# Transposing q and k by crossbar DMA in place of TensorE for five of eight batches, with VectorE and SyncE held to program order

## The chip, the cores and the metric

The kernel runs on one core of one Trainium2 chip. The metric is the device time of one execution in microseconds (us). A run is called slow when it lies over 1.5% above the fastest run of the same kernel; comparisons below use fast runs. A ratio is the mean time of one kernel's fast runs over that of the other's fast runs of the same rounds, so it is not quite the ratio of the medians quoted beside it. Profiles are single executions: their spans differ by a few us from the medians (the profiled execution of the kernel before took 405.14 us, 5 us over its median).

The core has five engines with their own instruction streams. Here PE (TensorE) multiplies matrices, DVE (VectorE) and ACT (ScalarE) work element by element, POOL (GpSimd) issues the loads that convert fp32 to bf16, and SP (SyncE) issues all other DMAs.

## The reference

Attention with a causal bias, then a token and a channel mixer; 8 batches, 8 heads, 576 positions, 64 elements per head.

```python
scores = q @ k.T / sqrt(64)                     # per batch and head, 576 x 576
cum    = cumsum(maximum(s, 0))
bias   = minimum(-(cum[:, None] - cum[None, :]), 0)
attn   = softmax(where(causal, -1e9, scores + bias))
x      = (attn @ v), heads side by side          # batch x 576 x 512
u      = x + (x.T @ U @ V).T                     # mixing along the sequence, rank 32
out    = u + maximum(u @ w_ch1, 0) @ w_ch2       # mixing along the channels, 512 -> 2048 -> 512
```

## The kernel before

A *pair* is two heads of one batch; there are 32 pairs, four per batch. For each pair the kernel makes a `slot`: q and k with their 64 elements on partitions 0 to 63, and four extra rows on partitions 64 to 67 that carry the bias. These *row loads* come from DRAM by a small DMA of SyncE. q and k are loaded with positions on 72 partitions, so they have to be transposed; TensorE does that with an identity matrix into PSUM, and VectorE copies the result into the slot.

```python
def transposes(n):                       # pair n
    b, hp = divmod(n, PB)                # PB = 4 pairs per batch
    slot = slots[n % NSLOT]              # NSLOT = 5
    if b > 0:
        nc.sync.dma_start(out=slot[D:KA, :, 0 : 2 * S], in_=rows_hbm[...])     # the row load
    for hh in range(2):
        tp = pwork()...                  # a PSUM bank
        for c, src in enumerate((q_t[b], k_t[b])):
            for t2 in range(4):
                nc.tensor.transpose(tp[:, c, t2, :], src[:, h, ds(t2 * 128, 128)], identity[:TP, :TP])
        ...                              # two copies into slot[0:D, hh]
        yield
```

The channel mixer is dense TensorE work. It is cut into steps by `yield`, and the loop over pairs takes a few such steps between the steps of the attention, so that TensorE always has something to do:

```python
for n in range(PB, NP + 2):
    b, hp = divmod(n, PB)
    if hp == 0 and 1 < b < B - 1:
        load(b + 1)                      # q, k, v of the next batch, by GpSimd
    if n + 1 < NP:
        run(transposes(n + 1))
    if n < NP:
        run(scores(n))
    if hp == 1 and b > FT:
        run(seqmix(b - 1)); fill.append(chanmix(b - 1))
    if PB < n <= NP:
        run(values(n - 1))               # x of the pair; for b >= 2 also a DMA transpose xT<-x_sb
    ...
in_program_order(tc, traced, [E.Pool, E.PE])
```

What is emitted in this order is not necessarily executed in it. A scheduler in the build may reorder the instructions of an engine where the data allow it, unless `in_program_order` chains them. In the kernel before, TensorE and GpSimd are chained to the end, ScalarE, VectorE and SyncE only up to the first mixing (`in_program_order(tc, traced, [E.DVE, E.Activation, E.SP])` just before the loop).

The softmax here doesn't subtract the row's maximum and nothing guards it: scores larger than these inputs give would overflow.

## Time and profile before

| | before |
|---|---|
| median time | 400.07 us (399.89 to 408.59, 4 runs) |
| span of the profiled run | 403.4 us |
| TensorE busy | 382.8 us (95%) |
| one batch in the steady part (four pairs and a mixer) | 41.2 us |
| eight small transposes (one head) | 0.26 us |

The page of the kernel before, busy time of each engine, and the shares of the chain of work that ended last:

```profile
PE 382.8 (95%) x3525; PEld 218.2 (54%) x3525; DVE 223.3 (55%) x484; ACT 201.0 (50%) x384; POOL 56.3 (14%) x79
...
PE 82%; DMA 10%; DVE 5%; POOL 1%; issue 1%; ACT 1%; DVEq 0%; ACTq 0%
```

The busy times in four stretches of the steady part (columns: stretch, its length, then busy us and instructions of each engine, the granted TensorE clock, the DMA share, GB/s):

```profile
99.00:140.00 41.00, 40.62 (x429) 24.31 (x427) 28.76 (x57) 25.43 (x51) 5.88 (x7) 1.00 0.93 96
140.00:180.00 40.00, 39.01 (x404) 22.84 (x405) 27.41 (x59) 21.97 (x45) 5.88 (x7) 1.00 0.92 98
180.00:220.00 40.00, 39.72 (x408) 23.40 (x407) 27.31 (x58) 21.98 (x44) 5.88 (x7) 1.00 0.92 103
220.00:260.00 40.00, 39.72 (x392) 23.16 (x390) 27.06 (x57) 21.04 (x42) 5.88 (x7) 1.00 0.98 103
```

TensorE is busy for practically all of each stretch, at clock 1.00; VectorE for 27 of 40 us. So TensorE sets the time here, and work taken from it should come back as time. What one head's transposes cost it is read from the timeline, not from busy sums, which count overlapped time twice (columns: start, length, engine and line, operation):

```profile
213.12 0.29 PE L239 MATMUL pwork<-identity,q_sd 72*128 72x72 bf16 x4
213.25 0.29 PE L239 MATMUL pwork<-identity,k_sd 72*128 72x72 bf16 x4
213.38 1.03 PE L454 MATMUL pwork<-w_sb,hT 128*128 128x512 bf16 x4
214.25 0.29 PE L239 MATMUL pwork<-identity,q_sd 72*128 72x72 bf16 x4
```

From the first transpose at 213.12 to the next mixer matmul at 213.38 it is 0.26 us.

The last lines to note are those that the prediction passed over: when the row load is requested, and when it is needed. SyncE's timeline has the request:

```profile
209.81 0.24 SPq L228 DMA_DIRECT2D slot_92<-rows_hbm  x1
```

TensorE's timeline has the first matmul that reads that slot afterwards:

```profile
256.56 0.42 PE L260 MATMUL pscore<-slot_92 68*128 68x128 bf16 x5
```

The scheduler had moved the row load up to about the moment at which the slot falls free, 46.8 us ahead of its use (36 to 55 us for all 28 row loads of this trace). Nothing in the program text asks for that.

### The profile page before, as it was taken

The page shows a single profiled execution, that of the slowest core. Times are in us where ns is not written, and L with a number is a line of the kernel's source. Part 1 is how long each engine was busy: PE and PEld are TensorE (multiplying, and loading weights), DVE is VectorE, ACT ScalarE, POOL GpSimd, SP SyncE. Part 2 cuts the span into 40 slices and gives each one's busy share as a digit, 9 for nine tenths or more (in the row PEclk, how much of TensorE's full clock was granted, in tenths as well). Part 3 has the DMA queues.
Part 4 walks back from the last instruction along what each step waited for, and adds up shares of the span by engine and source line. Part 5 has one row for each costly group of instructions (what it writes and reads, how often), then busy time and mean ns, then how long its engine had stood idle before and what let it go on. Part 6 is the DMA issues. An engine that isn't in the chain of part 4 may idle for free.

```text
span 403.4 us, 8541 instructions
## 1 busy us (share of the span) xinstructions
PE 382.8 (95%) x3525; PEld 218.2 (54%) x3525; DVE 223.3 (55%) x484; ACT 201.0 (50%) x384; POOL 56.3 (14%) x79
## 2 busy tenths in 40 slices
PE   7798998798999999999999999999999999999995
PEld 3575445465555556655555565555565554444442
DVE  7875124587756775667566856785678353002011
ACT  5552479551874358534853386328642930530710
POOL 5750023320230041003200230000000000000000
PEclk9758999999999999999999999999999999999999
DMA  5999999999399359837992599251224014301002
GB/s 76 169 211 207 151 93 102 134 151 105 61 153 111 73 97 137 79 72 112 147 80 72 100 151 70 63 122 21 19 70 120 18 34 130 80 18 69 19 26 79
DMA packets 94149, 38.33 MB, mean 95 GB/s; under 512 B 77150, under 2 KB 88446, under 8 KB 94110
## 3 DMA queue, kind: packets, MB, share of 16 engines
q0 software_dynamic: 53360, 18.44, 59.8%
q1 hardware_dynamic: 40750, 19.35, 26.7%
q8 instruction: 27, 0.44, 0.5%
q14 instruction: 12, 0.10, 0.1%
HBM read 37.51 MB, written 9.95 MB: 118 GB/s over the span
## 4 chain that ended last, share of the span: by engine, by line
PE 82%; DMA 10%; DVE 5%; POOL 1%; issue 1%; ACT 1%; DVEq 0%; ACTq 0%
PE pwork L454 29%; PE pwork L442 29%; PE pscore L260 10%; DMA k_sd<-in_k_dram 7%; PE pwork L323 6%; PE pwork L239 3%; DMA v_slot_102<-in_v_dram 2%; DVE o_sb L464 1%; PE pscore L151 1%; PE pwork L395 1%; DVE x_sb L333 1%; PE pwork L352 1%; DMA hT<-in_s_dram 1%; POOL v_slot_102 L193 1%; ACT pT_87 L271 0%
## 5 line engine op out<-in xcount | busy, mean ns | idle before, releaser
L454 PE MATMUL pwork<-w_sb,hT 128*128 128x512 bf16 x576 | 142.2, 381 | 0.2 <-ACT slot_96 L245 0.2
L442 PE MATMUL pwork<-uT,w_sb 128*128 128x512 bf16 x576 | 141.0, 379 | 0.6 <-ACT slot_96 L245 0.3
L449 ACT ACTIVATE hT<-pwork 128x512 bf16<-128x512 f32 x144 | 87.8, 609 | 107.7 <-PE pwork L442 107.1
L454 PEld LDWEIGHTS <-hT 128*128 128x128 bf16 x576 | 51.8, 98 | 49.1 <-issue 0.8
L442 PEld LDWEIGHTS <-w_sb 128*128 128x128 bf16 x576 | 50.6, 98 | 47.4 <-DVE uT L377 0.7
L464 DVE TENSOR_TENSOR o_sb<-pwork,u_sd 128x512 f32<-128x512 f32 x36 | 24.9, 692 | 63.8 <-PE pwork L454 62.6
L271 ACT ACTIVATE pT_87<-pscore 128x512 bf16<-128x512 f32 x32 | 19.3, 603 | 30.7 <-PE pscore L260 30.6
L333 DVE TENSOR_TENSOR x_sb<-pwork,rec 128x320 bf16<-128x320 f32 x64 | 31.3, 490 | 2.0
L271 ACT ACTIVATE pT_86<-pscore 128x512 bf16<-128x512 f32 x32 | 19.3, 603 | 19.5 <-PE pscore L260 19.4
L99 POOL DMA_DIRECT2D q_sd<-in_q_dram x10 | 8.1, 811 | 142.1 <-PE pwork L239 126.6
L245 DVE COPY slot_96<-pwork 64x576 bf16<-64x576 bf16 x22 | 17.4, 797 | 13.9 <-PE pwork L239 13.6
L272 DVE TENSOR_TENSOR pT_87<-pT_87,keep 128x512 bf16<-128x512 bf16 x32 | 13.2, 416 | 20.5 <-ACT pT_87 L271 20.5
L272 DVE TENSOR_TENSOR pT_86<-pT_86,keep 128x512 bf16<-128x512 bf16 x32 | 13.2, 414 | 18.5 <-ACT pT_86 L271 18.4
L239 PEld LDWEIGHTS <-q_sd 72*128 72x128 bf16 x256 | 16.3, 100 | 13.2 <-DMA q_sd<-in_q_dram 1.3
L239 PE MATMUL pwork<-identity,k_sd 72*128 72x72 bf16 x256 | 19.2, 201 | 4.2 <-DMA k_sd<-in_k_dram 4.2
L377 DVE TENSOR_TENSOR uT<-pwork,xT 128x256 bf16<-128x256 f32 (+6 forms) x54 | 19.4, 418 | 6.4 <-PE pwork L395 6.4
L323 PEld LDWEIGHTS <-pT_86 128*128 128x128 bf16 x480 | 19.0, 100 | 7.2 <-issue 2.0
L332 DVE RECIPROCAL rec<-pwork 128x5 f32<-128x5 f32 x64 | 12.2, 192 | 19.2 <-PE pwork L323 18.9
L284 ACT ACTIVATE pT_87<-pscore 128x512 bf16<-128x512 f32 x32 | 19.5, 610 | 6.2 <-PE pscore L260 6.2
L284 ACT ACTIVATE pT_86<-pscore 128x512 bf16<-128x512 f32 x32 | 19.5, 611 | 4.7 <-PE pscore L260 4.6
L245 DVE COPY slot_93<-pwork 64x576 bf16<-64x576 bf16 x26 | 20.6, 796 | 2.0 <-PE pwork L239 1.6
L323 PEld LDWEIGHTS <-pT_87 128*128 128x128 bf16 x480 | 18.8, 100 | 5.3 <-DVE pT_87 L297 0.3
(100 smaller groups left out, 441.3 us busy)
## 6 DMA issues: line engine op xcount, KB each, us to landing
out_dram<-o_sb SPq DMA_DIRECT2D x36, 256.0 KB
w_sb<-in_moe_w_ch_dram POOLq DMA_DIRECT2D x2, 2048.0 KB, 20.8
q_sd<-in_q_dram POOLq DMA_DIRECT2D x7, 576.0 KB, 8.4
k_sd<-in_k_dram POOLq DMA_DIRECT2D x7, 576.0 KB, 14.0
v_slot_102<-in_v_dram POOLq DMA_DIRECT2D x12, 128.0 KB, 13.5
v_slot_103<-in_v_dram POOLq DMA_DIRECT2D x12, 128.0 KB, 15.3
v_slot_104<-in_v_dram POOLq DMA_DIRECT2D x8, 128.0 KB, 17.6
rows_hbm<-hT SPq DMA_DIRECT2D x1, 504.0 KB
```

The source lines that it names most:

```text
L239: nc.tensor.transpose(tp[:, c, t2, :], src[:, h, ds(t2 * 128, 128)], identity[:TP, :TP])
L245: copy(dst[:, :, :, :, par], tp[par * D : par * D + D].rearrange("p c t m -> p c m t"),)
L260: nc.tensor.matmul(dst, lhsT=kT[:, ds(j * 128, 128)], rhs=qT[:, lo:hi], start=True, stop=True,)
L271: nc.scalar.activation(pT[:, hh, 0:512], diag, EXP, scale=scale)
L272: nc.vector.tensor_tensor(pT[:, hh, 0:512].rearrange("p (a b) -> p a b", a=4), pT[:, hh, 0:512].rearrange("p (a b) -> p a b", a=4), keep.t ...
L284: nc.scalar.activation(pT[:, hh, 512:1024], far, EXP, scale=scale)
L323: nc.tensor.matmul(po[:, i, :], lhsT=pT[:, hh, ds(place(j, i), 128)], rhs=vt[:, j, h, :], start=(j == 0), stop=(j == i), skip_group_check= ...
L333: nc.vector.tensor_tensor(x_sb[:, hp, :, ds(hh * D, D)], po[:, :, 0:D], rec.to_broadcast([128, 5, D]), op=ALU.mult,)
L442: nc.tensor.matmul(f1, lhsT=w1_sb[:, kt, ds(nf * 128, 128)], rhs=u[:, kt, :], start=(kt == 0), stop=(kt == 3),)
L449: nc.scalar.activation(hT[:, nf, :], f1, RELU)
L454: nc.tensor.matmul(f2, lhsT=hT[:, nf, ds(i * 128, 128)], rhs=w2_sb[:, nf, :], start=(nf == 0), stop=(nf == NF - 1),)
L464: nc.vector.tensor_tensor(o_sb.rearrange("p (a b) -> p a b", a=4), f2.rearrange("p (a b) -> p a b", a=4), u_sd[:, :, i, :], op=ALU.add,)
```

## The change

The intent: take 320 of the 512 small transposes off TensorE. From batch 3 on, one DMA per pair transposes q and k through the crossbar, three pairs ahead; q and k are loaded into two fixed buffers two batches ahead. VectorE and SyncE are chained to the end, so that the copies and fetches stay where they are written. The buffers have 80 partitions, not 72: "DMA: Bandwidth & Descriptors", section "DMA Transpose (X-bar)", of the Trainium skill asks for a multiple of 16; a small DMA fills the eight spare partitions once per buffer. In the same edit two small tiles of the mixing (`uxT` and `ux`) go from two buffers to one.

```diff
+    qks = [consts.tile([TR, H, 2, TT * D], BF16, name=f"qk{i}") for i in range(2)]     # TR = 80
+    def fetch(n):
+        b, hp = divmod(n, PB)
+        qkT_of[n] = work.tile([128, 2, 2, 4, TR], BF16, tag="qkT", name="qkT", bufs=3)
+        nc.sync.dma_start_transpose(
+            out=qkT_of[n].rearrange("p a c t m -> p (a c t) m"),
+            in_=qks[b % 2][:, ds(2 * hp, 2), :, :].rearrange("p h c x -> p (h c x)"))
 ...
+            if qkT is not None:
+                tp = qkT[:, hh, :, :, :TP]            # VectorE copies from here; no TensorE
+            else:
                 ... nc.tensor.transpose ...
 ...
-    in_program_order(tc, traced, [E.DVE, E.Activation, E.SP])
+    in_program_order(tc, traced, [E.Activation])
 ...
     for n in range(PB, NP + 2):
-        if hp == 0 and 1 < b < B - 1:
-            load(b + 1)
+        if hp == 0 and 1 < b < B - 1:
+            load_v(b + 1)
+        nb = b + 2
+        if hp == (1 if b >= QT else 3) and QT <= nb < B:      # QT = 3
+            load_qk(nb, 0, H)
+        if hp == 1 and QT - 2 <= b < QT:
+            nc.sync.dma_start(out=qks[b % 2][TP:], in_=qks[b % 2][2 * TP - TR : TP])
+        if QT * PB <= n + 3 < NP:
+            fetch(n + 3)
         if n + 1 < NP:
             run(transposes(n + 1))
 ...
-    in_program_order(tc, traced, [E.Pool, E.PE])
+    in_program_order(tc, traced, [E.Pool, E.PE, E.DVE, E.SP])
```

More of the change, by code (lines that the diff above doesn't have):

```diff
@@ L70 @@
     FT = 2
+    QT = 3
     consts = ctx.enter_context(tc.tile_pool(name="consts", bufs=1))
-    loads = ctx.enter_context(tc.tile_pool(name="loads", bufs=2))
     work = ctx.enter_context(tc.tile_pool(name="work", bufs=2))
@@ L89 @@
     nc.sync.dma_start(out=s_sb, in_=s.rearrange("b h s -> (b h) s"))
-    q_t, k_t = {}, {}
-    def alloc_qk(b):
-        q_t[b] = loads.tile([TP, H, TT * D], BF16, tag="q_sd", name="q_sd")
-        k_t[b] = loads.tile([TP, H, TT * D], BF16, tag="k_sd", name="k_sd")
+    TR = 80
+    qks = [consts.tile([TR, H, 2, TT * D], BF16, name=f"qk{i}") for i in range(2)]
     def load_qk(b, h, n):
-        for dst, src in ((q_t[b], q), (k_t[b], k)):
+        for c, src in enumerate((q, k)):
             nc.gpsimd.dma_start(
-                out=dst[:, ds(h, n), :],
+                out=qks[b % 2][:TP, ds(h, n), c, :],
                 in_=src[b, ds(h, n)].rearrange("h (p t) d -> p h (t d)", p=TP),
             )
-    alloc_qk(0)
     load_qk(0, 0, 2)
@@ L169 @@
             )
-    for dst in (q_t[0], k_t[0]):
-        nc.vector.memset(dst[:, 4:8, 0:2], 0.0)
+    nc.vector.memset(qks[0][:TP, 4:8, :, 0:2], 0.0)
     load_qk(0, 4, 4)
@@ L210 @@
     nc.gpsimd.dma_start(out=w2_sb, in_=moe_w_ch2.rearrange("(kt kp) n -> kp kt n", kp=128))
-    alloc_qk(1)
     load_qk(1, 0, H)
     load_v(1)
-    uT_of, x_of, xT_of = {}, {}, {}
+    uT_of, x_of, xT_of, qkT_of = {}, {}, {}, {}
     def uT(g):
@@ L220, in uT @@
         return uT_of[g]
+    def fetch(n):
[3 more added lines that the diff above has]
+            out=qkT_of[n].rearrange("p a c t m -> p (a c t) m"),
+            in_=qks[b % 2][:, ds(2 * hp, 2), :, :].rearrange("p h c x -> p (h c x)"),
+        )
     def transposes(n):
@@ L231, in transposes @@
             )
+        qkT = qkT_of.pop(n, None)
         for hh in range(2):
             h = 2 * hp + hh
-            tp = pwork().bitcast(BF16)[:, : 2 * 4 * TP].rearrange(
-                "p (c t m) -> p c t m", c=2, t=4
-            )
-            for c, src in enumerate((q_t[b], k_t[b])):
-                for t2 in range(4):
-                    nc.tensor.transpose(
-                        tp[:, c, t2, :], src[:, h, ds(t2 * 128, 128)], identity[:TP, :TP]
-                    )
+            if qkT is not None:
+                tp = qkT[:, hh, :, :, :TP]
+            else:
+                tp = pwork().bitcast(BF16)[:, : 2 * 4 * TP].rearrange(
+                    "p (c t m) -> p c t m", c=2, t=4
+                )
+                for c in range(2):
+                    for t2 in range(4):
+                        nc.tensor.transpose(
+                            tp[:, c, t2, :],
+                            qks[b % 2][:TP, h, c, ds(t2 * 128, 128)],
+                            identity[:TP, :TP],
+                        )
             dst = slot[0:D, hh, 0 : 2 * S].rearrange("p (c m t two) -> p c m t two", c=2, t=4, two=2)
@@ L359, in seqmix @@
                 )
-        uxT = work.tile([128, 128], BF16, tag="uxT", name="uxT")
+        uxT = work.tile([128, 128], BF16, tag="uxT", name="uxT", bufs=1)
         nc.vector.tensor_copy(uxT, up)
@@ L365, in seqmix @@
         nc.tensor.matmul(up, lhsT=uxT, rhs=identity, start=True, stop=True)
-        ux = work.tile([128, 128], BF16, tag="ux", name="ux")
+        ux = work.tile([128, 128], BF16, tag="ux", name="ux", bufs=1)
         nc.vector.tensor_copy(ux, up)
@@ L515 @@
         spin(2, pscore)
-    in_program_order(tc, traced, [E.DVE, E.Activation, E.SP])
-    def load(b):
-        alloc_qk(b)
-        load_qk(b, 0, H)
-        load_v(b)
-    load(2)
+    in_program_order(tc, traced, [E.Activation])
+    load_qk(2, 0, H)
+    load_v(2)
     fill.append(chanmix(0))
```

## The prediction

> **What bounds the kernel now.** TensorE. The page has PE busy 382.8 of 403.4 us; the chain of waits is 82% PE. Busy time in windows: 140 to 184 us PE 42.8 of 44, 184 to 225 40.7 of 41, 225 to 266 40.7 of 41, 266 to 308 41.7 of 42, 308 to 343 35.0 of 35; granted clock 1.00 in all. VectorE has 28 of 41 us in such a stage, ScalarE 22. Only 0 to 98 us differs (PE 40.7 of 45 between 40 and 85, DMA engines saturated by loads). So from about 98 us on, a microsecond less of PE work is a microsecond of time, unless a new wait appears.
>
> **What goes.** 16 small transposes of each of the 20 pairs of batches 3 to 7 (320 of 512). They are pipelined, so busy time overstates them: in the timeline eight transposes occupy 213.12 to 213.38 and again 214.25 to 214.50 us, and the next four 128x512 matmuls run at their usual 0.87 us. That is 0.257 us per head; 40 heads x 0.257 = 10.3 us, all where PE is saturated. The mixer's interleaving goes by yields, whose number stays, so PE's remaining order is the same.
>
> **What comes.** 20 crossbar transposes of 80 rows x 2048 columns from SyncE; 80, because a transpose wants a multiple of 16 partitions (Trainium skill, "DMA: Bandwidth & Descriptors", section "DMA Transpose (X-bar)"; no run here shows it). The present 128x2048 transpose, when alone, busies the DMA engines for about 2.6 to 3 us and takes SyncE 1.7 to 2.3 us to issue; the 128x640 one takes about 1.0 us alone, up to 4.6 us among batch loads. By rows, my estimate for the new one is 1.7 to 2 us alone, 4 to 9 us among loads, issue 1.5 us. Three pairs ahead is 27 us (a pair takes 8.9 us in the timeline), so it should be hidden. The DMA share of a steady batch is 0.9 of 41 us, but half of that is the load burst of 18 us; four more transposes, some 8 us, fit. The skill's "Advanced Engine Details and Errata", section "X-Bar Transpose (TRN2)", expects 350 to 400 GB/s of transposes; here the DMA view shows about 210 for them, against 369 to 410 for output stores.
> VectorE's copies (797 ns from PSUM) should take 650 to 750 ns from SBUF (estimate), uncritical.
>
> **Order and loads.** GpSimd's order of loads stays; q and k buffers are freed earlier by as much as they are needed earlier. First fetch at about 98 us; batch 3's q, k have landed by 91. Program order on VectorE and SyncE follows PE's program order: small waits at most, perhaps small gains (PE loses about 4 us to VectorE after 85 us). Risks: at each batch's second pair the last transpose of x meets the load burst and the new transposes, and the mixer's evacuation waits 1 to 2 us; SyncE, blocked in order by a late load, delays row loads.
>
> **Prediction.** 400.2 - 10.3 + 0 to 2 of new waits - 0 to 2 of better order: 390.0 us, range 387 to 394. Chances: faster by over 2% 0.78, within 2% 0.19, slower 0.03.
>
> **Right if:** 320 fewer PE matmuls; pairs of batches 3 to 7 take 8.4 us; PE still 99% busy there; the 60 us of pure mixer at the end unchanged; copies wait for no DMA. **Wrong if:** VectorE copies wait for the new transposes, PE falls under 97% in a steady stage, the first 100 us change by over 2 us, or crossbar transposes take over 15 us each.

## The result

The changed kernel took 425.43 us (median of 4 runs, 419.54 to 429.14; two of them slow) against 400.07: ratio of the fast runs 1.053, 95% interval 1.044 to 1.062. It is slower by 5%, not faster by 2.6%. Its page, busy time and chain:

```profile
PE 381.7 (91%) x3205; PEld 210.0 (50%) x3205; DVE 214.5 (51%) x483; ACT 201.2 (48%) x384; POOL 57.3 (14%) x79
...
PE 69%; DMA 17%; DVE 6%; ACT 3%; issue 2%; SPq 2%; POOL 1%; ACTq 0%; DVEq 0%
```

The same four stretches of the changed kernel:

```profile
99.00:140.00 41.00, 37.09 (x322) 20.58 (x320) 24.11 (x52) 20.84 (x42) 5.88 (x7) 0.92 1.04 121
140.00:180.00 40.00, 35.27 (x330) 19.58 (x329) 24.29 (x55) 22.07 (x44) 5.88 (x7) 1.00 1.11 127
180.00:220.00 40.00, 36.19 (x301) 19.66 (x300) 22.21 (x52) 19.16 (x39) 6.26 (x7) 0.91 1.16 124
220.00:260.00 40.00, 37.38 (x330) 20.67 (x329) 25.33 (x56) 19.89 (x39) 6.27 (x7) 1.00 1.11 136
```

There are 320 fewer matmuls, as intended. But over these 161 us TensorE is busy for 145.9 us, against 159.1 before: it now waits for 15 us, where it waited for 2. In two stretches the clock is lower as well. What it waits for, from the waits of PE over the whole run (columns: us in total, times, longest), the first line of the list:

```profile
PE pscore L269 <- DMA slot<-rows_hbm: 14.0, 7, 3.8
```

The longest of these waits, in the chain of waits (start, length, what):

```profile
124.67 0.31 PE pscore L269 x3
124.98 8.19 DMA slot<-rows_hbm
133.17 0.14 issue
133.31 0.64 PE pscore L269 x5
```

The scores of a pair wait for that pair's row load, a DMA of 18 KB whose own packets take under 1 us, but which landed 8.2 us after its request. In this trace row loads are requested 3 to 14 us before their scores from pair 10 on. SyncE's timeline around it:

```profile
120.04 1.31 SPq L349 DMA_TRANSPOSE xT<-x_sb  x1
121.40 3.49 SPq L222 DMA_TRANSPOSE qkT<-qk  x1
124.98 0.49 SPq L231 DMA_DIRECT2D slot<-rows_hbm  x1
...
129.93 4.78 SPq L222 DMA_TRANSPOSE qkT<-qk  x1
134.81 0.43 SPq L231 DMA_DIRECT2D slot<-rows_hbm  x1
```

The request of 124.98 comes after a crossbar transpose of x (120.04) and one of q and k (121.40), and the packet records show those two moving their 1920 rows of 256 bytes from 123.9 to 131.2 us; the eight packets of the row load move from 131.2 to 131.9, right behind them. That fits what "DMA: Bandwidth & Descriptors", section "Two DMAs through the same engine are not ordered", says of one queue of one DMA engine: its descriptors start in order. Also, issuing the crossbar transpose held SyncE for 3.5 and 4.8 us, where the median is 1.4. So the row load was requested late, and then stood in line.

The stall has a tail. TensorE's clock right after that wait:

```profile
129.00:133.00 4.00, 0.47 (x3) 0.00 (x0) 2.14 (x4) 0.00 (x0) 0.00 (x0) 0.99 2.02 144
133.00:140.00 7.00, 6.69 (x27) 3.23 (x28) 1.68 (x4) 2.45 (x5) 0.00 (x0) 0.52 0.72 102
140.00:143.00 3.00, 3.00 (x41) 1.92 (x40) 0.69 (x2) 1.08 (x2) 1.65 (x2) 1.00 0.56 96
```

After an idle gap of 3.8 us the clock was 0.52 for the next 7 us. "TensorE: Matmul & The Clock Gate", section "What's actually happening", has the array at half clock after an idle window of about 3.4 us; this gap agrees. But a shorter one did it as well: at 209.2 us, after a stretch without a pause, TensorE waited 2.8 us for a row load, and half clock followed.

```profile
205.00:209.20 4.20, 4.20 (x42) 2.09 (x38) 3.28 (x8) 2.99 (x7) 0.00 (x0) 1.00 1.43 147
209.20:212.00 2.80, 0.03 (x1) 0.00 (x0) 0.75 (x2) 0.60 (x1) 0.00 (x0) 0.90 1.30 158
212.00:218.00 6.00, 5.93 (x26) 3.06 (x27) 0.85 (x2) 3.15 (x6) 0.00 (x0) 0.50 0.29 57
```

### The profile page after: what moved, and what is told of

The parts are those of the page before. It is cut to its first block, busy times and chain, and to the rows that moved or that the text cites. A ratio compares the mean times of both kernels' runs of the same rounds, so it can differ in the third digit from the quotient of the medians.

```text
span 417.8 us, 7944 instructions
## 1 busy us (share of the span) xinstructions
PE 381.7 (91%) x3205; PEld 210.0 (50%) x3205; DVE 214.5 (51%) x483; ACT 201.2 (48%) x384; POOL 57.3 (14%) x79
## 4 chain that ended last, share of the span: by engine, by line
PE 69%; DMA 17%; DVE 6%; ACT 3%; issue 2%; SPq 2%; POOL 1%; ACTq 0%; DVEq 0%
PE pwork L463 26%; PE pwork L451 25%; DMA slot<-rows_hbm 11%; PE pscore L269 10%; PE pwork L332 5%; DMA xT<-x_sb 3%; DMA v_slot<-in_v_dram 3%; ACT pT L297 1%; DVE o_sb L473 1%; DVE x_sb L342 1%; PE pscore L148 1%; SPq L222 1%; PE pwork L404 1%; DVE slot L254 1%; DMA hT<-in_s_dram 1%
## 5 line engine op out<-in xcount | busy, mean ns | idle before, releaser
L269 PE MATMUL pscore<-slot 68*128 68x128 bf16 (+4 forms) x576 | 70.1, 257 | 15.6 <-DMA slot<-rows_hbm 14.0
L463 PEld LDWEIGHTS <-hT 128*128 128x128 bf16 x576 | 53.9, 100 | 55.7 <-issue 3.5
L269 PEld LDWEIGHTS <-slot 68*128 68x128 bf16 x576 | 45.8, 105 | 51.1 <-DMA slot<-rows_hbm 13.6
L280 ACT ACTIVATE pT<-pscore 128x512 bf16<-128x512 f32 x64 | 38.6, 603 | 63.7 <-PE pscore L269 63.5
L281 DVE TENSOR_TENSOR pT<-pT,keep 128x512 bf16<-128x512 bf16 x64 | 26.8, 422 | 60.6 <-ACT pT L280 59.8
L254 DVE COPY slot<-qkT 64x576 bf16<-64x576 bf16 x80 | 53.8, 672 | 0.8
L332 PEld LDWEIGHTS <-pT 128*128 128x128 bf16 x960 | 37.4, 100 | 15.3 <-DVE uT L386 3.4
L293 ACT ACTIVATE pT<-pscore 128x512 bf16<-128x512 f32 x64 | 39.0, 609 | 11.4 <-PE pscore L269 11.2
L332 PE MATMUL pwork<-v_slot,pT 128*128 128x65 bf16 x960 | 39.8, 197 | 3.1 <-DMA v_slot<-in_v_dram 1.4
L297 ACT ACTIVATE pT<-pscore 128x512 bf16<-128x512 f32 x64 | 39.4, 615 | 0.0
L254 DVE COPY slot<-pwork 64x576 bf16<-64x576 bf16 x36 | 28.3, 796 | 14.4 <-PE pwork L246 13.9
L189 POOL DMA_DIRECT2D v_slot<-in_v_dram x32 | 29.1, 924 | 11.4 <-DMA v_slot<-in_v_dram 6.1
L148 PE MATMUL pscore<-busy 128*128 128x512 bf16 (+1 forms) x53 | 19.6, 467 | 1.3 <-DVE busy L124 1.3
## 6 DMA issues: line engine op xcount, KB each, us to landing
w_sb<-in_moe_w_ch_dram POOLq DMA_DIRECT2D x2, 2048.0 KB, 19.7
```

The costliest lines, as they stand in the source:

```text
L189: nc.gpsimd.dma_start(out=vt[:, t, :, 0:D], in_=v[b, :, ds(t * 128, 128), :].rearrange("h p d -> p h d"),)
L254: copy(dst[:, :, :, :, par], tp[par * D : par * D + D].rearrange("p c t m -> p c m t"),)
L269: nc.tensor.matmul(dst, lhsT=kT[:, ds(j * 128, 128)], rhs=qT[:, lo:hi], start=True, stop=True,)
L280: nc.scalar.activation(pT[:, hh, 0:512], diag, EXP, scale=scale)
L293: nc.scalar.activation(pT[:, hh, 512:1024], far, EXP, scale=scale)
L297: nc.scalar.activation(pT[:, hh, 1024:1536], mid, EXP, scale=scale)
```

## The experiments

My theory A: the loss is SyncE's program order. Row loads, which the scheduler had placed four to five pairs ahead, are now one pair ahead and behind crossbar transposes. Rivals: B, the crossbar's traffic crowds the DMA engines, whatever the order; C, VectorE's program order makes it wait for copies or masks. All twelve runs gave correct results (e10 and e12 are the same file); each was timed beside the kernel before on the same chip in 3 rounds (the last in 5).

### e1: SyncE free again, VectorE in order

```diff
-    in_program_order(tc, traced, [E.Activation])
+    in_program_order(tc, traced, [E.Activation, E.SP])
-    in_program_order(tc, traced, [E.Pool, E.PE, E.DVE, E.SP])
+    in_program_order(tc, traced, [E.Pool, E.PE, E.DVE])
```

> The changed kernel, but SyncE is held to program order only as far as in the kernel before; VectorE stays in order to the end. Theory A (SyncE's program order puts each pair's row load behind a crossbar issue that blocks for 4 to 6 us under loads): row loads move up again, TensorE waits under 2 us for them, time 388 to 393. Theory B (the crossbar traffic itself crowds the DMA engines): still over 405. Theory C (VectorE's program order): still over 410.

Measured: 401.05 us (395.65 to 404.98, two of four runs slow), ratio 0.991 (0.984 to 0.999). Row loads are gone from TensorE's waits. Most of the loss came back, more than B or C allow, but not the 388 to 393 that A asked for: something else costs some us. (Its profile fell on a slow run and isn't used for time.)

### e2: the program order alone, without the crossbar

The kernel before, with the two `in_program_order` lines of the changed kernel.

> The kernel before with only the program order on VectorE and SyncE to the end, no crossbar transposes of q and k. Theory A: row loads come late here too, but only the issue of the x transposes stands before them, so a smaller loss, 400 to 408. Theory B: 399 to 401. Theory C: over 410.

Measured: 410.74 us, ratio 1.023 (1.019 to 1.027). Above A's 400 to 408, and just over the 410 that C asked for. Program order alone costs 2.3% of the kernel, with not one crossbar transpose of q and k. Two engines are chained here, so this doesn't say which. TensorE waited for a row load once:

```profile
PE pscore L260 <- DMA slot<-rows_hbm: 3.5, 1, 3.5
```

### e3: the crossbar with the order of before

```diff
-    in_program_order(tc, traced, [E.Activation])
+    in_program_order(tc, traced, [E.DVE, E.Activation, E.SP])
-    in_program_order(tc, traced, [E.Pool, E.PE, E.DVE, E.SP])
+    in_program_order(tc, traced, [E.Pool, E.PE])
```

> The changed kernel with the order of before (VectorE, ScalarE and SyncE held only to the end of the first mixing). Theory A: 388 to 394. Theory B: over 405. Theory C: 388 to 394.

Measured: 434.31 us, ratio 1.081 (1.075 to 1.086). A and C missed it; B's number is met, but not for B's reason. VectorE's waits (us in total, times, longest):

```profile
DVE slot L254 <- DMA qkT<-qk: 35.0, 2, 19.3
```

VectorE's timeline at the shorter of the two (the wait stands in brackets):

```profile
81.11 0.75 DVE L281 TENSOR_TENSOR pT<-pT,keep 128x512 bf16<-128x512 bf16 x2
97.57 0.65 DVE L254 COPY slot<-qkT 64x576 bf16<-64x576 bf16 x1 [15.71 <-DMA qkT<-qk]
```

The scheduler, not knowing how late the crossbar data come, moved the copies of batch 3 up among the work of batch 1; VectorE then stood for 15.7 us from 82 us on, and once for 19.3 us, and TensorE behind it. From e1 to e3 only VectorE's chain differs: ratio 0.991 against 1.081, and 397.8 against 433.6 us in the mean of the fast runs. So the change does need VectorE in order once the crossbar feeds it. That part of its design is right.

### e4: full program order, row loads written four pairs ahead

```diff
-        if b > 0:
-            nc.sync.dma_start(out=slot[D:KA, ...], in_=rows_hbm[...])      # in transposes(n)
+    def fetch_rows(n): ...                                                 # the same DMA
     for n in range(PB, NP + 2):
+        if n + 4 < NP:
+            fetch_rows(n + 4)                # that slot was last read by scores(n - 1)
```

(and the rows of pairs 4 to 7 ahead of the loop)

> The changed kernel with full program order, but each pair's row load is written four pairs ahead in the program, when its slot is already free. Theory A: TensorE's wait for row loads goes from 14 us to under 1 us, time 388 to 393. Theory B: over 405. Theory C: over 410.

Measured: 395.70 us (394.54 to 397.13), ratio 0.986 (0.982 to 0.991). One small DMA moved up takes the ratio from 1.053 to 0.986. TensorE waits for no row load of this kind at all. This is the main cause, shown by undoing it. Of what remains over the predicted 390, a part shows in VectorE's waits between 98 and 330 us:

```profile
DVE slot L255 <- DMA qkT<-qk: 3.7, 1, 3.7
...
DVE uT L387 <- DMA xT<-x_sb: 2.0, 1, 2.0
```

And in the chain of waits:

```profile
207.40 13.48 DMA xT<-x_sb
```

A crossbar transpose of x, requested at 207.40, landed 13.5 us later, in the time of a load burst. This wait held TensorE up for 1.6 us:

```profile
PE pwork L452 <- DVE uT L387: 1.6, 1, 1.6
```

Where the other 4 us or so went isn't shown by this trace.

### e5: the crossbar fetch two pairs ahead

```diff
-        if hp == (1 if b >= QT else 3) and QT <= nb < B:
+        if hp == (2 if b >= QT else 3) and QT <= nb < B:
             load_qk(nb, 0, H)
-        if QT * PB <= n + 3 < NP:
-            fetch(n + 3)
+        if QT * PB <= n + 2 < NP:
+            fetch(n + 2)
```

(on top of e4)

> e4 with the crossbar fetch two pairs ahead in place of three, so that a batch's last fetch, which frees the q and k buffer for the next load, is issued after that batch's last x transpose. If the rest of e4's loss is the mixer waiting for x transposes that meet the load burst, VectorE's wait for them goes to under 0.5 us, the batches take 39.1 us each from batch 3 on, and the time is 390 to 393. If it is the amount of crossbar traffic whatever its timing, it stays at 394 to 397; if two pairs are too short, VectorE waits for the fetches and it is over 397.

Measured: 428.54 us, ratio 1.065 (1.060 to 1.070). My idea for an improvement was wrong, and the run says why:

```profile
DVE slot L255 <- DMA qkT<-qk: 42.1, 5, 11.6
```

VectorE stood five times, for 42 us in all, before the copies. In the packet records, a train of crossbar transposes that meets a load burst (5143 rows of 256 bytes: one of u, two of x and one of q and k, and a part of the next) took 19.7 us, 153.3 to 172.9, or 3.8 ns per row; the same records have the transpose of x alone at 640 rows in 0.95 us, 1.5 ns per row. And the lead is shorter than it is called. The copies of a pair are written one step ahead of its scores, so a fetch "three pairs ahead" has two steps to land: in the changed kernel the first fetch is issued at 103.1 us and its copies begin at 119.9, 16.8 us later. "Two pairs ahead" leaves one step, some 8 to 10 us. A train of 20 us is just beyond the first (e4 waited 3.7 us once) and far beyond the second.

### e6: the row load just before the fetch, still one pair ahead

The changed kernel with `fetch_rows(n + 1)` placed in front of `fetch(n + 3)`.

> The changed kernel with one swap: the next pair's row load stands just before the crossbar fetch of the same step, still one pair ahead. If the crossbar issue in front of the row load is the main part of the loss, 395 to 405. If one pair of lead is too short in itself, over 412.

Measured: 419.09 us, ratio 1.047 (1.040 to 1.054). So it isn't the fetch of the same step that does the harm: one pair of lead is too little as long as SyncE's queue carries this many crossbar transposes. The chain of waits shows the worst case:

```profile
157.94 7.31 DMA slot<-rows_hbm
```

Here the row load, first of its step, stood behind a transpose of u (issued 147.31) and one of x (154.31).

### e7 and e11: which engine's order costs without the crossbar

e7 is e2 with row loads four pairs ahead. e11 is e7 with VectorE chained only to the first mixing, as before:

```diff
-    in_program_order(tc, traced, [E.Activation])
+    in_program_order(tc, traced, [E.DVE, E.Activation])
-    in_program_order(tc, traced, [E.Pool, E.PE, E.DVE, E.SP])
+    in_program_order(tc, traced, [E.Pool, E.PE, E.SP])
```

> e2 (the kernel before with program order to the end, no crossbar of q and k) with row loads four pairs ahead. If late row loads are all that program order costs there, 399 to 402. If VectorE's order costs by itself, over 405.

> e7 with VectorE's order as in the kernel before; SyncE stays in program order to the end with row loads four pairs ahead, no crossbar transposes of q and k. If VectorE's program order is what e7 still loses, 399 to 402 and TensorE's waits for x_sb between 60 and 99 us back from 4.4 to about 1.2 us. If SyncE's order still costs with rows early, 405 to 408.

Measured: e7 407.39 us, ratio 1.017 (1.013 to 1.022); e11 400.50 us, ratio 0.995 (0.990 to 1.001). So SyncE's program order costs nothing that these runs can see once the row loads are written early, and VectorE's costs about 7 us (407.39 - 400.50; 9 us by the two ratios). Late row loads cost some 3 us here (e2 against e7, 410.74 - 407.39; the intervals of the two ratios overlap), where some 27 us were lost with the crossbar: the late request and the crossbar in front of it make the loss together. TensorE's waits between 60 and 99 us in e7:

```profile
PE pwork L240 <- DVE x_sb L334: 2.1, 2, 1.2
PE pwork L353 <- DVE x_sb L334: 1.6, 1, 1.6
...
PE pwork L455 <- DVE x_sb L334: 0.7, 1, 0.7
```

The same of e11:

```profile
PE pwork L353 <- DVE x_sb L334: 1.0, 1, 1.0
...
PE pwork L240 <- DVE x_sb L334: 0.3, 1, 0.3
```

The compiled order tells why. In program order VectorE does the second mask of a pair (which waits for ScalarE's last exponential) and only then the x of the pair before, which TensorE is waiting to see evacuated; the scheduler had swapped them:

```
e7:   mask 128x512 x2, mask 128x2x64, reciprocal, x_sb, reciprocal, x_sb, copy ...
e11:  mask 128x512 x2, reciprocal, x_sb, mask 128x2x64, reciprocal, copy, x_sb ...
```

The waits named account for 3 of the 7 us (4.4 against 1.3). By the start of the third batch's mixing e7 is 6.0 us behind e11, by the fourth's 7.3, and by the end 7.8: in these two traces nearly the whole loss is in the first 180 us. How the other 4 us divide wasn't taken apart, and one of these stretches, the first row of the last table, differs by 5 us between two executions of one file (e10 and e12).

### e8, e9, e10 and e12: towards a version that keeps the gain

e8 is e4 with VectorE free between the first mixing and the start of batch 2, chained after that. e9 is e4 with the loads cut: when a pair has been fetched, only its part of the buffer is refilled, and a part of v with it, so that one burst per batch becomes four small ones. e10 is both; e12 is the same file as e10 in 5 rounds.

```diff
+        if n == 2 * PB:
+            ordered = len(nc.cur_bb.bb.instructions)                   # e8
-    in_program_order(tc, traced, [E.Pool, E.PE, E.DVE, E.SP])
+    in_program_order(tc, traced, [E.Pool, E.PE, E.SP])                 # e8, with E.DVE to the first mixing
+    in_program_order(tc, ordered, [E.DVE])
 ...
             fetch(n + 3)
+            fb, fp = divmod(n + 3, PB)                                 # e9
+            if fb + 2 < B:
+                load_qk(fb + 2, 2 * fp, 2)
+            if fb + 1 < B:
+                load_v(fb + 1, ((0,), (1,), (2,), (3, 4))[fp])
```

> e4 with VectorE free of program order between the first mixing and the start of batch 2 (as in the kernel before), in order after that. If program order on VectorE costs the 3 us of extra TensorE waits for x_sb seen between 60 and 99 us in e4 and e7, those waits fall from 4.6 to about 1.5 us and the time falls by 2 to 4 us against e4, to 391 to 394. If those waits are hidden or replaced, 394.5 to 397.

> e4 with the loads of q, k (from batch 5 on, and batch 4 in three parts) and v (from batch 4 on) cut into parts by pairs of heads, each released when its own pair's buffer has been fetched, so that one load burst of 18 us per batch becomes four small ones. If the load burst is what makes crossbar transposes slow, a train of them no longer takes 17 to 20 us, VectorE's wait for x transposes falls from 2 us to under 0.5 us, and the time is 391 to 394.5. If crossbar transposes crowd each other whatever the loads do, 395 to 398.

> e8 and e9 together. If both causes are real and separate, the gains add: 388 to 392, TensorE at 39.1 us per batch from batch 3 on and at least 2% faster than the kernel before. If they are one cause, no better than the better of the two.

> The same file as e10, more rounds, for a firmer interval: 390 to 393 against 400 to 402, a ratio of 0.970 to 0.982.

| kernel | median us | ratio | 95% interval |
|---|---|---|---|
| e4 | 395.70 | 0.986 | 0.982 to 0.991 |
| e8 | 394.36 | 0.984 | 0.978 to 0.990 |
| e9 | 394.62 | 0.985 | 0.980 to 0.990 |
| e10 | 392.11 | 0.976 | 0.970 to 0.982 |
| e12 | 393.12 | 0.976 | 0.969 to 0.983 |

e8, e9, e10 and e12 all land within a microsecond above the range that was hoped for; e12's ratio is inside it. Neither e8 nor e9 differs from e4 by more than the intervals, so neither part alone is shown to help; both fell between the two outcomes that were expected for them. In e8's trace TensorE's waits for x_sb between 60 and 99 us did fall, from 4.6 us in e4 to 1.9. The two parts together (e10, e12) are faster than the kernel before by 2.4%; the 2% line is still inside the interval. In e9's, e10's and e12's traces VectorE waits for no crossbar transpose; in e8's the wait for x is absent too, but 5.0 us of waits for q and k are there. In e4 a wait of this sort cost TensorE only 1.6 us in the profiled run (the line shown above), so e9 had little to win by itself.

The four stretches of e12:

```profile
99.00:140.00 41.00, 39.62 (x392) 22.74 (x391) 29.39 (x66) 22.50 (x45) 15.76 (x23) 1.00 1.44 156
140.00:180.00 40.00, 39.71 (x359) 22.33 (x357) 27.01 (x61) 22.68 (x47) 11.20 (x15) 1.00 1.44 156
180.00:220.00 40.00, 39.71 (x357) 22.42 (x356) 26.28 (x60) 22.87 (x47) 12.04 (x15) 1.00 1.27 148
220.00:260.00 40.00, 39.51 (x353) 22.05 (x352) 25.76 (x59) 22.73 (x46) 0.00 (x0) 1.00 0.49 97
```

TensorE is busy 97 to 99% of each stretch again, at full clock, with 37 to 51 fewer matmuls per stretch than before.

The pace in one table: time from one batch's first mixing matmul to the next batch's, read from the TensorE timelines (us).

| mixing of batch | before | after | e4 | e12 |
|---|---|---|---|---|
| 0 to 1 | 56.1 | 57.7 | 55.1 | 51.0 |
| 1 to 2 | 48.0 | 55.7 | 47.0 | 47.0 |
| 2 to 3 | 39.3 | 41.0 | 37.2 | 37.2 |
| 3 to 4 | 41.2 | 46.0 | 39.1 | 39.1 |
| 4 to 5 | 41.2 | 41.8 | 41.0 | 39.1 |
| 5 to 6 | 41.1 | 39.4 | 39.4 | 39.4 |

In the steady part a batch takes 2.1 us less wherever nothing waits: 41.2 to 39.1, eight heads of 0.26 us each, as the prediction reckoned. In the last row the loads are over (the changed kernel's last ended at 254 us), and there even the changed kernel has 39.4. The first row can't be read in this way: e10 is the same file as e12, and its trace has 55.9 there in place of 51.0. So the 5 us between before and e12 in that row are not shown to come from the change; from the third row to the sixth their difference is 8.0 us.

## Why the prediction was wrong

- **What bounds the kernel, and what the transposes cost: right.** The gain per batch was reckoned as 8 x 0.257 = 2.06 us and is 2.1 us in e4, e8, e9, e10 and e12. TensorE was the bound, and still is in those versions.
- **The step that failed: "Program order on VectorE and SyncE follows PE's program order: small waits at most".** It was sized at 0 to 2 us. SyncE's order, as written, puts the row loads one pair ahead and behind crossbar transposes; moving them four pairs ahead (e4) takes the ratio from 1.053 to 0.986, which is 6.7% of about 400 us, some 27 us, the clock's drop after stalls included. VectorE's order cost about 7 us in the kernel without the crossbar (e7 against e11); what it costs in the changed kernel isn't measured apart. I had both lines in the profile of before: SyncE's row load at 209.81 for a slot used at 256.56, and the program text that asks for it one pair ahead. I compared the new order with TensorE's, and not with the order that the scheduler had made.
- **"SyncE, blocked in order by a late load, delays row loads": the right victim, the wrong cause and size.** In the changed kernel no late load was needed (batch 4's q and k, for one, landed at 127.6 us and were fetched from 146.3 us on); the crossbar transposes themselves blocked it, by their issue (up to 6.1 us, reckoned as 1.5) and in the queue (8.2 us to land for the row load at 124.98).
- **"4 to 9 us among loads" for one new transpose, "so it should be hidden": half right.** "Three pairs ahead is 27 us" was a miscount: it is two steps, 16.8 us where measured. They are nearly hidden there, in e4 with 3.7 us of VectorE's waits. But transposes come in trains with those of x and u, and a train among loads took up to 20 us. With one step less (e5) that cost about 32 us against e4 (ratio 1.065 against 0.986). The lead in the change was not generous, it was needed.
- **The signs of error that were named.** TensorE's share did fall under 97% in the steady part (37.09 of 41 us is 90%). VectorE's copies waited for no new transpose in the changed kernel's trace: the danger that was guarded against wasn't the one that came. "The first 100 us change by over 2 us" stays undecided: at the second batch's mixing the changed kernel was 2.2 us behind (93.1 against 90.9), but e10 and e12, one file, differ by 3.6 us at the same place (88.6 and 85.0). By the third's mixing it was 9.9 us behind (148.8 against 138.9).
- **VectorE's copies: right.** They take 672 ns in the mean from SBUF, 796 from PSUM.

Theory B holds for a smaller part: a load burst does slow crossbar transposes, by 2.5 times per row in e5, and that decides how much lead is needed; it doesn't make the change slow by itself, since e12 moves the same bytes. Theory C is right in the direction but has two sides: VectorE's program order costs about 7 us where no crossbar data are waited for, and saves about 36 us (e3 against e1) where they are.

Left open: how 4 of VectorE's 7 us come about; what keeps e1 and e4 above 390 us beyond the waits named; and e12's spread, 389.3 to 398.5 us in six runs, of which two count as slow.

## What to carry to other kernels

When an engine is held to program order, compare the program with the order that the scheduler had made, instruction by instruction, on that engine: a DMA request that it had moved up has to be written early by hand (four pairs ahead, when the slot is free, was enough here). A request for a small transfer waits in its queue behind the large ones, so its lead has to cover the longest train in front of it, not its own duration. And an order imposed to protect one stage is best tried from that stage on: VectorE's chain was needed once there were crossbar data (e3), and cost time without them (e7 against e11). That beginning it later helps by itself is not shown (e8 against e4), only that together with the smaller loads (e10, e12) it has the best times.

## What the Trainium skill lacked or had wrong

- "Advanced Engine Details and Errata", section "X-Bar Transpose (TRN2)", expects 350 to 400 GB/s and calls transposes as fast as regular DMAs. Here a 128x640 bf16 transpose alone took 0.95 us for 160 KB (about 170 GB/s), and one of 128x2048 took 2.6 us for 512 KB (about 200 GB/s); an output store of 256 KB took 0.82 us by the same count (about 320 GB/s; the 369 to 410 of the prediction are single slices of the DMA view). Transposes of other shapes or sizes were not tried.
- No page tells what a transpose costs next to converting loads of GpSimd: 3.8 ns per row of 256 bytes in a train of 5143, against 1.5 ns alone.
- "DMA: Bandwidth & Descriptors", section "Issuing engines are not separate DMA queues", calls the time to initiate a DMA usually small relative to the DMA itself. For crossbar transposes of q and k SyncE was held 1.4 us in the median, where one alone moved its data in 2.0 us, and up to 6.1 us under loads (8.7 us for u), and all its later requests with it.
- The same page tells that descriptors of a queue start in order, but not what follows for planning: an 18 KB load landed after 8.2 us behind two transposes.
- "TensorE: Matmul & The Clock Gate", section "What's actually happening", gives about 3.4 us of idle time for the drop to half clock. In the changed kernel's trace a gap of 2.8 us was enough (0.50 from 212 to 218 us), and one of 2.1 us at 254.7 us was not.
